# Attention and two mixers on one core: zadd and umm moved ahead of the odd tile's transposes, the last z step one place later, the last output in halves

## The chip, the cores and the metric

One core of a Trainium2 chip runs the whole program once. The metric is device time in microseconds (us) of that core, the median of several executions. The engines are PE (TensorE), VectorE (DVE), ScalarE (ACT), GpSimd (POOL) and SyncE (SP), which mostly issues DMAs. TensorE writes only to PSUM, which this program uses as one tile `ps` of eight banks of 512 float32 columns.

## The reference

Clustered attention, then two mixers. Batch 2, 8 heads, 768 tokens, 64 columns a head.

```python
mask = q_assign[:, :, :, None] == k_assign[:, :, None, :]        # argmax over 16 centroids
scores = np.where(mask, scale * np.matmul(q, k.transpose(0, 1, 3, 2)), -1000000000.0)
attn = np.exp(scores - np.max(scores, axis=-1, keepdims=True))
x = np.matmul(attn / (np.sum(attn, axis=-1, keepdims=True) + 1e-09), v)
# mixer 1: x as (2, 768, 512); U is (768, 32), V (32, 768): a token mix of rank 32
u = x + (x.transpose(0, 2, 1) @ U @ V).transpose(0, 2, 1)
x = u + np.maximum(u @ w_ch1, 0.0) @ w_ch2                       # 512 -> 2048 -> 512
# mixer 2: token mix through 256 with a ReLU, then channels 512 -> 1536 -> 512
u = x + (np.maximum(x.transpose(0, 2, 1) @ w_tok1, 0.0) @ w_tok2).transpose(0, 2, 1)
return u + np.maximum(u @ w_ch1, 0.0) @ w_ch2
```

## The kernel before, in words

Heads go in pairs: 4 pairs in each of 2 batches, 8 groups of 12 tiles, so tiles n = 0 to 95, 128 queries of one head against 768 keys each. The order of the work on each engine is written out by hand: `step(n)` issues the instructions of tile n, and tables (`mid`, `low`, `acts`, `late`) hold what else goes into a step, by tile number. `at(table, n, f)` puts f there. Two tiles, an even and the following odd one, make a pair of steps:

- Even n: score heads of tile n+2 (`s_mm`, four matmuls), `mid`, four of tile n's transposes, VectorE's maximum of tile n+2 (`s_max`), the other two transposes, ScalarE's exponential of tile n+1 (`s_exp`), a copy of four finished transposes to SBUF (`t_out`, ScalarE), `late`.
- Odd n: two transposes, the heads and the maximum of tile n+2, four transposes, `mid`, a `t_out` on VectorE, eight PV matmuls of an earlier half group, `low`, `acts`, the exponential of n+1, a `t_out` on ScalarE, `late`.

Scores lie in banks 0 to 3. Transposes and all extra work take banks 4, 5 and 6 in turn from `ring()`: each taker gets the bank taken three takers before, and must wait until its reader is done. Bank 7 collects PV. `merge` transposes a finished half group back, `merge_out` divides it by its sums into `xn`, the attention's output.

The low-rank token mix of batch 0 is done inside attention of batch 1. `zmm` (tile 59) is x^T U, `zmm_out` copies its four pieces to `z32` (L360), `z_split` makes three parts of it in `zst` (two roundings on ScalarE, L78; one subtraction on VectorE, L85), `zadd` multiplies one block of 128 tokens by V (six blocks, tiles 65, 69, 71, 75, 77, 81), and `zadd_out` adds it to `xn` (L373). `umm` transposes a block of the sum (L377; tiles 83, 87, 89, 93), and `umm_out` splits it into a rounded high part on ScalarE (L78) and the low rest on VectorE (L85): `uh` and `ul`, the input of the channel mixer. `wide` converts weight blocks of the first mixer meanwhile (L96 to L109).

After tile 95 the channel mixer runs in units k: `hidden(k)` (12 matmuls, bank 4 or 5), `hidden_out(k)` (ReLU high part `gh` on ScalarE, low part `gl` on VectorE), `outmm(k)` (12 matmuls into banks 0 to 3). `half_slots` issues hidden(k+1), hidden_out(k+1) and outmm(k) in turn, one slot each. Between the slots `rest_of_u` does the z and u work of the remaining blocks: a list `ops` of pairs (PE part, reader part) which takes banks 6 and 7 in turn. Before the PE part of ops[i] it issues the reader part of ops[i-1]; then it lets some slots pass, by a table of numbers, (1, 1, 2, 2, 1, 1, 1) for the first seven. ops[0] is umm of token block 4, and `zmm` of batch 1 is put in at place 1; its reader part is `z_last` (copies by VectorE and ScalarE in turn, then `z_split`). At the very end `outmm` adds the residual (L750) and sends each of four blocks out by a DMA on SP (L752).

Of the kernel before, what the change touches and what calls it, by code (L numbers as in the profile page):

```python
# [24 lines left out]
def tile_cluster_attention__then__two_mixers(  # L25
# [24 lines left out]
    pe, dve, act, pool, sp = nc.tensor, nc.vector, nc.scalar, nc.gpsimd, nc.sync  # L50
    NB, NPAIR, _, S = qT.shape
# [5 lines left out]
    NC = CD // P  # L57
# [4 lines left out]
    G = NB * NPAIR  # L62
    NTT = 4 * NT
    TW = 512
    NPASS = NB * S // TW
# [6 lines left out]
    def mm(o, l, r, start, stop, **kw):  # L72
        pe.matmul(o, lhsT=l, rhs=r, start=start, stop=stop, **kw)  # L73

    def rnd(eng, o, i, scale=1.0):

        if eng is act:
            act.activation(o, i, AF.Copy, scale=scale)  # L78
        elif eng is dve and scale == 1.0:
            dve.tensor_copy(o, i)  # L80
        else:
            eng.tensor_scalar(out=o, in0=i, scalar1=scale, scalar2=1.0, op0=ALU.mult, op1=ALU.mult)
# [105 lines left out]
    held = {}  # L188
# [115 lines left out]
    def ring():  # L304

        banks.append(banks.pop(0))
        return banks[-1]

    def t_mm(n, c0, c1):
        for c in range(c0, c1):  # L310
            j, i = divmod(NS * n + c, 4)
            if i == 0:
                tb[j] = ring()
            pe.transpose(ps[:, tb[j], ts(i, P)], p32[n % NP32][:, ts(c, P)], ident)  # L314
# [13 lines left out]
    def pv_out(q):  # L328
        act.copy(osb[q % 2], ps[:, OB, 0:HS])

    def merge(q, bk=None):
        held["mg"] = bk = bk or ring()
        for t in range(NT):
            pe.transpose(ps[:, bk, ts(t, P)], osb[q % 2][:, ts(t, P)], ident)  # L334
# [12 lines left out]
    def zmm(gs, bk):  # L347
        held["z"] = bk
        for c in range(NS):
            for i, g in enumerate(gs):  # L350
                b, p = divmod(g, NPAIR)
                mm(ps[R * i : R * i + R, bk, 0:P], u_sb[:, c, :], xn[:, b, p, c, :], c == 0, c == NS - 1)

    def zmm_out(gs, engs):
        for i, g in enumerate(gs):
            z, o = ps[R * i : R * i + R, held["z"], 0:P], z32[:, ts(g % NPAIR, P)]
            if engs[i % 2] is act:
                act.copy(o, z)
            else:
                dve.tensor_copy(o, z)  # L360

    def z_split(gs):
        n, g = len(gs), gs[0]
        z, o = z32[:, g % NPAIR * P : (g % NPAIR + n) * P], zst[:, g * P : (g + n) * P]
        return [lambda: rnd(act, o[0:32], z), lambda: rnd(act, o[32:64], z), lambda: sub(dve, o[64:96], z, f32(o[0:32]))]
# [5 lines left out]
    def zadd_out(b, t, bk):  # L371
        o = xn[:, b, :, t, :]
        dve.tensor_tensor(out=o, in0=ps[:, bk, :].rearrange("p (c k) -> p c k", c=NC), in1=o, op=ALU.add)  # L373
# [5 lines left out]
    def umm_out(b, t, bk):  # L379
        p, k = divmod(b * S + t * P, TW)  # L380
        uh, ul = (x[:, :, k : k + P] for x in fst["u"][p])
        o = ps[:, bk, :].rearrange("p (c k) -> p c k", c=NC)
        return [lambda: rnd(act, uh, o), lambda: sub(dve, ul, o, f32(uh))]
# [178 lines left out]


    NTILE = G * NTT
    mid, low, acts, late = {}, {}, {}, {}

    def at(d, s, f):
        d.setdefault(max(s, 0), []).append(f)

    for g in range(G):  # L570
        s0 = NTT * g
        for h in range(2):
            s = s0 + 2 * NT * h + 4 * NT + 1
            at(mid, s, lambda q=2 * g + h: merge(q))
            at(late, s, lambda q=2 * g + h: merge_out(q))
        n, s1 = g + 1, s0
# [13 lines left out]
            at(late, s1 + 6 if n > 1 else 4, lambda g=n: load_v(g))  # L590

    at(low, 59, lambda: zmm(range(NPAIR), ring()))
    at(late, 60, lambda: zmm_out(range(NPAIR), (dve, dve)))
    for d, s, f in zip((acts, acts, late), (61, 63, 64), z_split(range(NPAIR))):
        at(d, s, f)

    for t in range(NS):
        s = (65, 69, 71, 75, 77, 81)[t]

        def za(t=t):  # L600
            held["za"] = ring()
            zadd(0, t, held["za"])

        at(mid, s, za)
        at(late, s if s == 69 else s + 1, lambda t=t: zadd_out(0, t, held["za"]))
    for s, f in ((0, arg0), (1, lambda: arg1(pool)), (2, arg2), (3, lambda: arg3(pool)), (4, arg4), (5, lambda: mask_rows(pool))):
        at(late, s, f)
    for a in range(2):
# [15 lines left out]
    for t in range(TW // P):  # L624

        def um(t=t):
            held["um"] = ring()
            umm(0, t, held["um"])

        s = NTILE - (13, 9, 7, 3)[t]  # L630
        at(mid, s, um)
        at(acts, s, lambda t=t: umm_out(0, t, held["um"])[0]())
        at(late, s + 1, lambda t=t: umm_out(0, t, held["um"])[1]())

    def step(n):
        k, r = divmod(n, 2 * NT)
        j, i = divmod(NS * n, 4)

        def run(d):
            for f in d.get(n, ()):  # L640
                f()

        def heads():
            if n + 2 < NTILE:
                s_mm(n + 2)

        def maxima():
            if n + 2 < NTILE:
                s_max(n + 2)

        def exps():
            if n + 1 < NTILE:
                s_exp(n + 1)

        def pvs():
            if k:
                pv(k - 1, r - 1)
                pv(k - 1, r)

        def pvo():  # L660
            if k and r == 2 * NT - 1:
                pv_out(k - 1)

        if i == 0:
            heads()
            run(mid)
            t_mm(n, 0, 4)
            maxima()
            t_mm(n, 4, NS)
            exps()  # L670
            t_out(j)
            pvo()
            run(late)
        else:
            t_mm(n, 0, 2)
            heads()
            maxima()
            t_mm(n, 2, NS)
            run(mid)
            t_out(j)  # L680
            pvs()
            run(low)
            run(acts)
            exps()
            t_out(j + 1)
            pvo()
            run(late)
# [41 lines left out]
    def outmm(k):  # L729
        m, p, f = units[k]  # L730
        lo, hi = next(x for x in spans(m, p) if x[0] <= f < x[1])
        wh, wl = (weights(k)[:, 1, j, :] for j in range(2))
        gh, gl = fst["g"][0][k % 2], fst["g"][1][k % 2]
        for c in range(NC):
            o = ps[:, c, :]
            cs = ts(c, P)
            mm(o, wh[:, cs], gh, f == lo, False)
            mm(o, wh[:, cs], gl, False, False)
            mm(o, wl[:, cs], gh, False, f == hi - 1)
        uh, ul = fst["u"][p]  # L740
        if lo == 0 and f == hi - 3:

            for b, s, n, k in pieces(p * TW, TW):
                for c in range(NC):
                    dve.tensor_tensor(out=x2[b][:, c, s : s + n], in0=f32(uh[:, c, k : k + n]), in1=f32(ul[:, c, k : k + n]), op=ALU.add)
        if f == hi - 1:
            for c in range(NC):
                for b, s, n, k in pieces(p * TW, TW):
                    o = x2[b][:, c, s : s + n]
                    dve.tensor_tensor(out=o, in0=ps[:, c, k : k + n], in1=o, op=ALU.add)  # L750
                    if m:
                        sp.dma_start(out[b, c][:, s : s + n], o)  # L752


    def pieces(s0, n, size=S):
        i, k = s0, 0
        while k < n:
            b, s = divmod(i, size)
            w = min(size - s, n - k)
            yield b, s, w, k  # L760
            i, k = i + w, k + w
# [8 lines left out]
    last = 2 * G - 1  # L770
# [5 lines left out]
        pv(last, c)  # L776
    pv_out(last)
    hidden(0, (3,))
    merge(last, 6)
    merge_out(last)  # L780
    ap_ctx.close()

# [88 lines left out]
    def rest_of_u():  # L871


        def z_last(bk):
            gs = range(NPAIR, G)
            zmm_out(gs, (dve, act))
            for f in z_split(gs):
                f()

        def u_out(b, t, bk):  # L880
            for g in umm_out(b, t, bk):
                g()

        u_, z_ = ([(f, o, b, t) for b in range(NB) for t in range(NS)] for f, o in ((umm, u_out), (zadd, zadd_out)))
        ops = []
        order = u_[4:6] + z_[6:8] + u_[6:8]
        for i in range(8, 12):
            order += z_[i : i + 1] + u_[i - 1 : i] * (i > 8)
        order.append(u_[11])
        for f, o, b, t in order:  # L890
            ops.append((lambda bk, f=f, b=b, t=t: f(b, t, bk), lambda bk, o=o, b=b, t=t: o(b, t, bk)))
        ops.insert(1, (lambda bk: zmm(range(NPAIR, G), bk), z_last))
        for i in range(len(ops) + 1):
            if i:
                ops[i - 1][1](6 + (i - 1) % 2)
            if i < len(ops):
                ops[i][0](6 + i % 2)
            for _ in range((1, 1, 2, 2, 1, 1, 1)[i] if i < 7 else 4 if i > 7 else 12):
                yield
# [74 lines left out]
```

## Time and profile before

| | |
|---|---|
| three runs | 768.66, 767.53, 767.29 us; median 767.53 |
| the profiled execution | 767.95 us, its span 766.2 us |
| busy: PE, VectorE, ScalarE, GpSimd | 738.7, 467.1, 310.1, 166.4 us |
| granted TensorE clock | 1.000 of full speed |

In the rows below L73 is the line of all plain matmuls, L314 the transposes of tiles, L334 merge, L377 umm, L292 the maximum, L297 the exponential. A count behind x tells how many instructions a row merges. In a timeline a bracket at the end of a row tells how long the engine was idle before, and what ended that. A row's duration of a few matmuls is longer than the distance to the next row, since matmuls overlap; the chain of waits gives distances.

### The profile page before, as it was taken

To read this page: it belongs to the slowest core of one execution; us is meant where nothing else is said; L and a number is where in the kernel's file an instruction comes from. 1 tells how busy PE (TensorE), PEld (TensorE's weight loads), DVE (VectorE), ACT (ScalarE), POOL (GpSimd) and SP (SyncE) were. 2 spreads that over 40 slices of the span, in tenths; PEclk is the share of its full clock that TensorE was granted. 3 is DMA by queue.
4 is the path that set the end of the run, shared out by engine and by line. 5 is a ranking of instruction groups with operands and counts; after the bars stand their busy time and mean duration, and the time that the engine had idled before them with its cause. 6 is when DMAs were issued, how large, how long until landed. Compare 5 with 4: busy or idle time off the path is not lost.

```text
span 766.2 us, 10466 instructions
## 1 busy us (share of the span) xinstructions
PE 738.7 (96%) x3845; PEld 582.1 (76%) x3845; DVE 467.1 (61%) x689; ACT 310.1 (40%) x565; POOL 166.4 (22%) x147
## 2 busy tenths in 40 slices
PE   1899999999999999999999999999999999999998
PEld 0667766766666688888888888888888888888886
DVE  6778988877777366875758587666675432122113
ACT  3777877867776343332232324323232311111010
POOL 3321432421310122321322122125211410000000
PEclk9999999999999999999999999999999999999999
DMA  5886777875311344753632699967885647555652
GB/s 152 191 185 185 179 186 188 243 183 134 87 63 55 112 165 151 287 193 138 220 131 89 222 346 368 337 238 259 283 286 215 214 144 274 192 192 195 243 192 83
DMA packets 51714, 149.38 MB, mean 195 GB/s; under 512 B 7792, under 2 KB 15984, under 8 KB 49616
## 3 DMA queue, kind: packets, MB, share of 16 engines
q1 hardware_dynamic: 51152, 148.01, 59.7%
q10 hardware_dynamic: 512, 0.72, 0.3%
q8 instruction: 30, 0.49, 0.3%
q14 instruction: 20, 0.16, 0.1%
HBM read 97.32 MB, written 32.51 MB: 169 GB/s over the span
## 4 chain that ended last, share of the span: by engine, by line
PE 92%; DVE 3%; DMA 2%; ACT 2%; issue 1%; SPq 0%; ACTq 0%; DVEq 0%
PE ps L73 82%; PE ps L314 7%; DVE nm L292 1%; DMA xn<-in_U_dram 1%; ACT p L297 1%; ACT qk L78 1%; PE ps L377 1%; PE ps L822 1%; PE ps L334 1%; DMA sq__81<-in_qT_dram 1%; DMA qk<-om 0%; SPq L476 0%; DVE u_sb L100 0%; DVE xn L373 0%; DVE qk L85 0%
## 5 line engine op out<-in xcount | busy, mean ns | idle before, releaser
L727 DVE SCALAR_TENSOR_TENSOR gl<-ps,gh 128x512 fp32r<-128x512 f32 x84 | 58.0, 691 | 209.6 <-ACT gh L726 209.6
L73 PE MATMUL ps<-gh,qk 128*128 128x512 f32 x544 | 179.6, 391 | 0.1
L726 ACT ACTIVATE gh<-ps 128x512 fp32r<-128x512 f32 x84 | 50.2, 598 | 312.9 <-PE ps L73 311.5
L73 PE MATMUL ps<-qk 112*128 112x384 f32 (+2 forms) x456 | 110.8, 370 | 13.0 <-DMA qk<-om 10.3
L73 PEld LDWEIGHTS ps<-gh,qk 128*128 128x128 f32 x544 | 102.1, 188 | 21.6 <-issue 0.5
L292 DVE TENSOR_REDUCE nm<-ps 128x1 f32<-128x768 f32 x96 | 91.8, 956 | 41.5 <-PE ps L73 38.8
L73 PEld LDWEIGHTS ps<-qk 112*128 112x128 f32 (+1 forms) x456 | 77.2, 192 | 44.5 <-issue 20.7
L73 PE MATMUL ps<-gl,qk 128*128 128x512 f32 x272 | 106.1, 390 | 0.0
L85 POOL TENSOR_TENSOR qk<-c__77,qk 128x512 fp32r<-128x512 f32 x40 | 54.9, 1381 | 197.0 <-ACT qk L78 169.1
L297 ACT ACTIVATE p<-ps,nm 128x768 f32<-128x768 f32 x96 | 86.6, 902 | 7.4 <-DVE nm L292 6.8
L314 PE MATMUL ps<-ident,p 128*128 128x128 f32 x576 | 82.1, 275 | 2.6 <-DVE z L360 0.6
L314 PEld LDWEIGHTS ps<-ident,p 128*128 128x128 f32 x576 | 67.6, 140 | 12.8 <-ACT p L297 2.6
L73 PE MATMUL ps<-u2h,qk 128*128 128x512 f32 x224 | 73.9, 391 | 0.0
L73 PE MATMUL ps<-pt,vr 128*64 128x384 f32 x384 | 72.1, 498 | 0.0
L321 ACT COPY pt<-ps 128x512 f32<-128x512 f32 x96 | 56.1, 584 | 35.1 <-PE ps L314 34.7
L73 PEld LDWEIGHTS ps<-gl,qk 128*128 128x128 f32 x272 | 51.1, 188 | 10.2
L73 PE MATMUL ps<-u1h,qk 128*128 128x512 f32 x160 | 52.6, 390 | 0.0
L100 DVE TENSOR_SCALAR c__77<-c__77 128x512 f32<-128x512 f32 (+2 forms) x47 | 49.1, 1045 | 0.8 <-ACT c__77 L96 0.7
L73 PEld LDWEIGHTS ps<-u2h,qk 128*128 128x128 f32 x224 | 42.1, 188 | 8.6
L109 DVE SCALAR_TENSOR_TENSOR c__77<-c__76,c__77 128x512 int32<-128x512 int32 (+2 forms) x47 | 43.4, 923 | 1.5
L106 DVE SCALAR_TENSOR_TENSOR c__77<-c__76,c__77 128x512 int32<-128x512 int32 (+2 forms) x47 | 43.5, 925 | 1.1
L73 PE MATMUL ps<-u2l,qk 128*128 128x512 f32 x112 | 43.6, 390 | 0.0
(146 smaller groups left out, 1017.0 us busy)
## 6 DMA issues: line engine op xcount, KB each, us to landing
qk<-scr_b SPq DMA_DIRECT2D x72, 512.0 KB, 4.2
c__76<-in_wa_dram SPq DMA_DIRECT2D x16, 1024.0 KB, 4.8
qk<-scr_a SPq DMA_DIRECT2D x32, 512.0 KB, 7.6
c__76<-in_wb_dram SPq DMA_DIRECT2D x24, 512.0 KB, 5.1
scr_b<-qk SPq DMA_DIRECT2D x24, 512.0 KB, 4.2
scr_a<-wx SPq DMA_DIRECT2D x16, 512.0 KB, 2.9
scr_a<-qk SPq DMA_DIRECT2D x16, 512.0 KB, 2.7
qk<-sq__81 SPq DMA_DIRECT2D x14, 384.0 KB, 4.0
```

The lines of the kernel that those rows point to most:

```text
L73: pe.matmul(o, lhsT=l, rhs=r, start=start, stop=stop, **kw)
L78: act.activation(o, i, AF.Copy, scale=scale)
L85: eng.tensor_tensor(out=o, in0=a, in1=b, op=ALU.subtract)
L100: dve.tensor_scalar(out=dst, in0=dst, scalar1=2.0 ** -15, scalar2=122879.9921875, op0=ALU.max, op1=ALU.min)
L106: dve.scalar_tensor_tensor(out=d, in0=lo, scalar=29, in1=d, op0=ALU.logical_shift_right, op1=ALU.bitwise_or)
L109: dve.scalar_tensor_tensor(out=d, in0=hi, scalar=-0x40000000, in1=d, op0=ALU.bitwise_and, op1=ALU.bitwise_or)
L292: dve.tensor_reduce(out=nm[:, n % 4 : n % 4 + 1], in_=ps[:, b0 : b0 + 2, 0:HS], axis=AX.XY, op=ALU.max, negate=True)
L297: act.activation(p32[n % NP32].rearrange("p (j k) -> p j k", j=2), ps[:, b0 : b0 + 2, 0:HS], AF.Exp, bias=nm[:, n % 4 : n % 4 + 1], accum_ ...
L314: pe.transpose(ps[:, tb[j], ts(i, P)], p32[n % NP32][:, ts(c, P)], ident)
L321: act.copy(o, ps[:, tb[j], :])
L726: act.activation(gh, o, AF.Relu)
L727: dve.scalar_tensor_tensor(out=gl, in0=o, scalar=0.0, in1=f32(gh), op0=ALU.max, op1=ALU.subtract)
```

## The change

A new table `first` runs at the beginning of an odd step. zadd and umm of batch 0 move there from `mid`, which in an odd step stood behind all transposes. Their VectorE readers move from `late` to `mid` of the next even step, ahead of that step's maximum, and so do the copies after zmm in step 60. The first of z_split's roundings goes from step 61 to 63. The last merge takes bank 0 instead of 6, `zmm` of batch 1 goes to place 2 of `ops`. In the second mixer output DMAs alternate between SP and ScalarE, and the last block of the last pass goes out in two halves.

```diff
-    mid, low, acts, late = {}, {}, {}, {}
+    first, mid, low, acts, late = {}, {}, {}, {}, {}
...
-    at(late, 60, lambda: zmm_out(range(NPAIR), (dve, dve)))
-    for d, s, f in zip((acts, acts, late), (61, 63, 64), z_split(range(NPAIR))):
+    at(mid, 60, lambda: zmm_out(range(NPAIR), (dve, dve)))
+    for d, s, f in zip((acts, acts, late), (63, 63, 64), z_split(range(NPAIR))):
...
-        at(mid, s, za)
-        at(late, s if s == 69 else s + 1, lambda t=t: zadd_out(0, t, held["za"]))
+        at(first, s, za)
+        at(mid, s + 1, lambda t=t: zadd_out(0, t, held["za"]))
...
-        at(mid, s, um)
+        at(first, s, um)
         at(acts, s, lambda t=t: umm_out(0, t, held["um"])[0]())
-        at(late, s + 1, lambda t=t: umm_out(0, t, held["um"])[1]())
+        at(mid, s + 1, lambda t=t: umm_out(0, t, held["um"])[1]())
...
         else:
+            run(first)
             t_mm(n, 0, 2)
...
             for c in range(NC):
-                for b, s, n, k in pieces(p * TW, TW):
+                ends = list(pieces(p * TW, TW))
+                if m and p == NPASS - 1 and c == NC - 1:
+                    ends = [(b, s + i * n // 2, n // 2, k + i * n // 2) for b, s, n, k in ends for i in range(2)]
+                for b, s, n, k in ends:
...
-                        sp.dma_start(out[b, c][:, s : s + n], o)
+                        (sp, act)[(c + k // (TW // 2)) % 2].dma_start(out[b, c][:, s : s + n], o)
...
-    merge(last, 6)
+    merge(last, 0)
...
-        ops.insert(1, (lambda bk: zmm(range(NPAIR, G), bk), z_last))
+        ops.insert(2, (lambda bk: zmm(range(NPAIR, G), bk), z_last))
```

How it moves the instructions, first on PE in tiles 64 and 65 (p_0 and p_1 are their exponentials, zst and vst the operands of zadd):

```order
 L73 MATMUL ps<-qk_73 128x384 x4
 L314 MATMUL ps<-ident,p_0_91 128x128 x6
-L314 MATMUL ps<-ident,p_1_92 128x128 x2
-L73 MATMUL ps<-qk_73 128x384 x4
-L314 MATMUL ps<-ident,p_1_92 128x128 x4
 L73 MATMUL ps<-zst,vst 128x512
+L314 MATMUL ps<-ident,p_1_92 128x128 x2
+L73 MATMUL ps<-qk_73 128x384 x4
+L314 MATMUL ps<-ident,p_1_92 128x128 x4
 L73 MATMUL ps<-pt,vr_89 64x384 x4
```

zadd now stands between the last transpose of the even tile and the first of the odd one; the other five zadds and the four umms move in the same way.

On PE at the end of attention (L334 is the last merge, wx_75 is in hidden(1), xn,u_sb is zmm of batch 1, gh_2241 the beginning of outmm(0)):

```order
 L334 MATMUL ps<-ident,osb_97 128x128 x3
-L377 MATMUL ps<-ident,xn 128x128 x4
+L377 MATMUL ps<-ident,xn 128x128 x8
+L73 MATMUL ps<-qk_72,wx_75 128x512 x12
 L73 MATMUL ps<-xn,u_sb 32x128 x24
-L73 MATMUL ps<-qk_72,wx_75 128x512 x12
-L377 MATMUL ps<-ident,xn 128x128 x4
 L73 MATMUL ps<-gh_2241,wx_74 128x512
```

Two umms now come first, and zmm stands behind hidden(1). What follows on PE is the same in both: outmm(0), hidden(2), zadd of batch 1, outmm(1).

On ScalarE at the same place, before (gh_2241 is the ReLU of hidden_out(0), gh_2242 that of hidden_out(1), then gh_2241 again that of hidden_out(2); L358 are z_last's copies):

```order
L726 ACTIVATE gh_2241<-ps 128x512
L78 ACTIVATE u1h<-ps 128x4x128
L96 ACTIVATE c__77<-c__76 128x1024
L726 ACTIVATE gh_2242<-ps 128x512
L358 COPY z_110<-ps 32x128 x2
L78 ACTIVATE zst<-z_110 32x512 x2
L78 ACTIVATE qk_73<-c__77 128x2x512
L726 ACTIVATE gh_2241<-ps 128x512
```

and with the change:

```order
L727 ACTIVATE gh_2241<-ps 128x512
L78 ACTIVATE u1h<-ps 128x4x128
L96 ACTIVATE c__77<-c__76 128x1024
L727 ACTIVATE gh_2242<-ps 128x512
L78 ACTIVATE u1h<-ps 128x4x128
L78 ACTIVATE qk_73<-c__77 128x2x512
L727 ACTIVATE gh_2241<-ps 128x512
L358 COPY z_110<-ps 32x128 x2
L78 ACTIVATE zst<-z_110 32x512 x2
```

The copies and roundings of z_last stood behind the ReLU of hidden_out(1) and now stand behind that of hidden_out(2); VectorE's part moved in the same way.

## Rows read from the trace of the kernel before

**Rows 1.** The page, busy time of each engine over the span.

```profile
PE 738.7 (96%) x3845; PEld 582.1 (76%) x3845; DVE 467.1 (61%) x689; ACT 310.1 (40%) x565; POOL 166.4 (22%) x147
```

**Rows 2.** Chain of waits, in order of time: start, us, what; opening transposes of four pairs.

```profile
74.82 0.88 PE ps L314 x8
...
153.33 0.87 PE ps L314 x8
...
158.47 0.88 PE ps L314 x8
...
244.75 0.87 PE ps L314 x8
```

**Rows 3.** Chain of waits: matmul pieces between two holes, with their counts.

```profile
160.51 3.81 PE ps L73 x60
...
171.85 2.35 PE ps L73 x12
...
186.00 3.35 PE ps L73 x21
...
191.54 2.57 PE ps L73 x13
...
246.75 0.45 PE ps L377 x4
```

**Rows 4.** Timelines: a hole of PE in tile 61, and VectorE's work before it.

```profile
166.51 0.66 PE L314 MATMUL ps<-ident,p 128*128 128x128 f32 x4 [0.63 <-DVE z L360]
...
165.29 1.17 DVE L360 COPY z<-ps 32x128 f32<-32x128 f32 x4
```

**Rows 5.** Timelines of PE and VectorE in tiles 64 and 70.

```profile
174.03 1.04 PE L314 MATMUL ps<-ident,p 128*128 128x128 f32 x8
...
174.30 0.96 DVE L292 TENSOR_REDUCE nm<-ps 128x1 f32<-128x768 f32 x1 [0.77 <-PE ps L73]
175.29 0.68 DVE L85 TENSOR_TENSOR zst<-z,zst 32x512 fp32r<-32x512 f32 x1
...
189.20 1.20 PE L314 MATMUL ps<-ident,p 128*128 128x128 f32 x8
...
189.03 0.65 DVE L373 TENSOR_TENSOR xn<-ps,xn 128x512 f32<-128x512 f32 x1
```

**Rows 6.** Chain of waits: the transposes of tile 95.

```profile
250.12 0.88 PE ps L314 x6
```

**Rows 7.** Timeline of all engines after attention.

```profile
261.00 0.66 PE L377 MATMUL ps<-ident,xn 128*128 128x128 f32 x4 [0.71 <-DVE xn L342]
...
263.86 0.68 DVE L85 TENSOR_TENSOR u1l<-ps,u1h 128x512 fp32r<-128x512 f32 x1
...
265.89 0.60 PE L377 MATMUL ps<-ident,xn 128*128 128x128 f32 x4
...
266.25 0.48 PE L73 MATMUL ps<-gh,wx 128*128 128x512 f32 x1
...
269.19 0.68 DVE L85 TENSOR_TENSOR zst<-z,zst 32x512 fp32r<-32x512 f32 x1 [0.99 <-ACT zst L78]
...
271.82 0.39 PE L73 MATMUL ps<-zst,vst 96*128 96x512 f32 x1
```

**Rows 8.** PE timeline after two early waits; stretch by engine: busy (count), then granted clock.

```profile
19.03 2.90 PE L73 MATMUL ps<-qk 112*128 112x384 f32 x8 [9.70 <-DMA qk<-om]
...
28.12 0.98 PE L73 MATMUL ps<-qk 128*128 128x384 f32 x4 [1.98 <-ACT p L297]
...
19.00:24.00 5.00, 4.97 (x21) 3.42 (x22) 2.58 (x4) 3.56 (x6) 0.47 (x1) 1.00 0.56 112
```

**Rows 9.** The chain's last row; DMA issues of the output: KB, us to landing.

```profile
762.51 0.69 DVE xn L750
...
out_dram<-xn SPq DMA_DIRECT2D x8, 256.0 KB, 2.1
...
out_dram<-xn SPq DMA_DIRECT2D x8, 128.0 KB, 1.8
```

## The prediction, made before the changed kernel had run

> **What bounds the kernel now.** The page first: PE is busy for 96% of the span, the other engines for 61% at most [rows 1]. So time is won or lost only where PE's order of work has a hole, or where the end hangs on something else. Second the chain of waits, for the 17 pairs of tiles from the opening transposes of tile 58 to those of tile 92: 244.75 - 158.47 = 86.28 us. Tiles 22 to 56 are 17 pairs too, with no z or u work: 153.33 - 74.82 = 78.51 us [rows 2]. They have one set of cluster scores more, 3.35 - 2.57 = 0.78, so plain work is 77.73. To it come, from neighbouring pieces of the chain [rows 3], zmm at 3.81 - 2.35 = 1.46, six zadds at 2.57 - 2.35 = 0.22 and three umms at 0.45: 81.86 us. **The other 4.42 us are holes.** [Rows 4] show one kind: PE waits 0.63 in tile 61 for VectorE's four z copies (1.17 from 165.29), which stood behind a maximum. A second is zadd_out behind other work of VectorE: at 189.20 the transposes of tile 70 open, and a bank of theirs is read until 189.68 [rows 5]. A third kind lies in the umm pairs: ScalarE's rounding waits for a umm that PE reaches last in the odd tile, and the next exponential stands behind it.
>
> Third the timeline of the stretch after attention [rows 7] and the last rows [rows 9].
>
> **The change, part by part.** The sum is made against the profiled execution, 767.95 us (its span is 766.2); the median of the three runs is 767.53, 0.42 lower.
>
> *Pairs 58 to 91.* zadd and umm move ahead of the odd tile's eight transposes and score heads, their VectorE readers ahead of the next even tile's maximum. The bank that the odd tile's last four transposes take was then read in the tile before by a ScalarE copy, long done; umm has its result some 1.5 us earlier (four heads 0.9 [rows 8], six transposes 6/8 of 0.88), so ScalarE rounds while PE goes on. In tile 60 the four z copies start as zmm ends and no longer behind a maximum; that maximum starts a little later, and its exponential is wanted by PE only in tile 62. I take all 4.42 as gone. The lower bound is half of it, were exponentials late instead; there is no more than all of it above.
>
> *Three waits that come instead.* (1) zadd of tile 65 needs the last part of zst, which VectorE still makes after the maximum of tile 66: maximum from 174.30, subtraction 175.29 to 175.97 [rows 5]. PE opens the pair at 174.03 and now reaches zadd after six transposes, at 174.69. It stands until 175.97 + 0.04 = 176.01: **1.32 us**. Behind it stand all PE work and, through the heads, VectorE and ScalarE. (2) zadd_out of tile 69 still stands behind the scores' transpose; it ended at 189.03 + 0.65 = 189.68 [rows 5]. The transposes of tile 70 opened at 189.20 and wanted its bank with the fifth; now the first wants it, so they wait to 189.72, **0.52**. (3) In tile 72 zadd_out stands behind q_lo, which I estimate at **0.2** by the like order of (2). Sum 2.04 (1.3 to 2.6). By the opening of tile 92 the change has won 4.42 - 2.04 = 2.4.
>
> *Tiles 92 to 95.* No heads are left to cover for waits. From 246.75 PE's own work to the opening of tile 95 is umm 0.45, eight PV matmuls 1.45 (the 2.35 of rows 3 less four heads) and six transposes 0.66: 249.31, where the chain has 250.12 [rows 6]. Some 0.15 stays, for the bank that u's low half frees (maximum, copy and subtraction follow each other on VectorE). With the slow restart after the wait (0.88 for six against 0.66) the gain is 0.8, so 3.2 so far (1.0 to 3.9 by the bounds of the 4.42 and of the three waits, one at a time).
>
> *The end of attention* [rows 7]. merge's bank 0 removes the 0.71 that the first umm waited for the merge's reader. But zmm, now third, takes the first umm's bank and waits for u1l, which ends at 263.86 + 0.68 = 264.54, since VectorE's conversions of a weight block stand before it. zmm then runs 264.58 to 266.04, and the first output matmuls start at 266.04 instead of 266.25: 0.2 won.
>
> The other side of this edit is the largest single term. z_last (four copies, two roundings, a subtraction) now stands behind hidden_out(2) on both engines, and zadd of batch 1 stands on PE right behind hidden(2), ahead of outmm(1). So PE must stand from the end of hidden(2) until hidden_out(2) **and** z_last are done. Before, the same chain hung on hidden(1): from 265.89, when PE was done with it, to 269.19 + 0.68 + 0.04 = 269.91, **4.02 us**; it was hidden by outmm(0) and hidden(2), 5.57 us of PE work. That cover is gone. I see nothing on the queues that shortens or lengthens it much (3.7 to 4.4). hidden(2) ends 0.2 earlier for the gain at zmm, so zadd starts at 271.82 - 0.21 + 4.02 = 275.63 against 271.82: **3.8 lost** after this place. From there on the order is the same, and PE has no slack to win anything back.
>
> *The end* [rows 9]. Two half sums pay the start of an instruction twice and so end a little later than one whole of 0.69, I take 0.1, and a 128 KB piece lands in 1.8 after its issue, a 256 KB one in 2.1: 0.2 won (0 to 0.4). The Trainium skill (Trainium Kernel Development and Optimization, Key Constraints) says that DMAs from several queues share the same 16 engines and save only the issue time; by that rule this term is nearer 0, and the sum 0.2 higher. The other output DMAs on ScalarE wait for sums that end while PE does the next hidden matmuls, whose ReLU is the next thing on that queue: nothing. On SP only the output issues are fewer; its loads keep their order.
>
> Sum: -3.2 + 3.8 - 0.2 = **+0.4** (the 0.2 won at zmm is in the 3.8), so 768.35 for an execution like the profiled one, **767.9** at the median. A measurement of this kernel can tell about 0.2% (1.5 us) from no change; this is within it.
>
> **The rivals.**
>
> *Slower: PE comes out of the 4 us stand at half pace.* After its 9.70 us wait at the start PE took 2.90 us for eight matmuls of the kind that went four in 0.98 after a wait of 1.98, and 4.97 us for 21 matmuls [rows 8], where 21 like ones took 3.35 [rows 3]: 1.6 us lost. The granted clock reads 1.00 (2.4 GHz) there, but the pace is that of the lower level, 1.2 GHz. A stand of 4.02 lies nearer to 1.98 than to 9.70, so this is not the likeliest. It decides if PE falls after a stand somewhere between the two. Time: 767.9 + 1.6 = 769.5. The Trainium skill (TensorE: Matmul & The Clock Gate, HAM oscillation) warns that waits of a matmul stream for its data let the array's clock be throttled again, and tells of a kernel where each such wait did so; by it this rival would be the forecast. The trace agrees for 9.70 and shows nothing between.
>
> *Slower: the reordered VectorE queue only trades waits.* If the earlier sums delay maxima and with them exponentials, half of the 4.42 stays: 767.9 + 2.2 = 770.1. Against it: the maximum that starts later is an even tile's, and its exponential is wanted only after the rest of the pair's work and the next heads. That includes the case that the change doesn't do what it says; at tile 69 it does not, the reader keeps its place.
>
> *Faster: VectorE gets ahead.* If VectorE, with readers done early, came to its queue's next work sooner than I reckon, most of waits (1) to (3) would vanish, 1.5 us, and if the four z copies, which take 1.17 on one engine [rows 4], ran in two pairs side by side in z_last, 0.6 of the 4.02 would go too: 767.9 - 2.1 = 765.8. Against: wait (1) hangs on a maximum that hangs on PE itself, and in both kernels the copies of z_last take turns on the two engines.
>
> **How the numbers follow.** Forecast 0.55, with a range of its own of 766.6 to 769.0 from the bounds of its terms; PE at half pace 0.27; traded waits 0.06; faster 0.12. Of the forecast's share 0.04 lies beyond 0.2% slower (769.06), and of the half-pace case 0.06 within it; of the faster case 0.02 stays above 766.0. So slower 0.31, within 0.59, faster 0.10. The range 766.3 to 769.8 leaves out some 0.1 on each side.
>
> **What would show it.** Right: PE's transposes in the odd tiles without VectorE waits, tile 92 opened 2 to 3 us earlier against tile 58; a PE wait of about 1.3 for zst in tile 65 and 0.5 in tile 70; a PE wait of about 4.0 between hidden(2) and zadd of batch 1, one of the three longest of the kernel; the last output landing 0.2 earlier. Wrong: no wait at zadd of batch 1 (then 764), or matmuls behind it that take twice as long (then 769.5).

## The result, and the profile after

| | before | changed |
|---|---|---|
| median of six runs each, in turns | 767.35 us (766.90 to 768.66) | **771.54 us** (770.46 to 772.66) |
| ratio | | **1.0052, interval 1.0039 to 1.0065** |
| profiled execution, its span | 767.95, 766.2 us | 770.79, 769.0 us |

The change makes the kernel 4.2 us (0.5%) slower. Forecast was 767.9, "within 0.2%", and the range of 766.3 to 769.8 does not hold the result. The page hides all of it: the busy times [rows 1] are what they were.

```profile
PE 739.1 (96%) x3845; PEld 584.2 (76%) x3845; DVE 468.8 (61%) x690; ACT 310.6 (40%) x565; POOL 167.6 (22%) x147
```

So the difference has to be looked for in PE's order of work, stretch by stretch. The two traces side by side, in us; tile 58 is taken at its opening transposes, hidden(n) and outmm(n) at their first matmul in PE's timeline:

| stretch | before | changed | difference | predicted |
|---|---|---|---|---|
| start to tile 58 | 158.31 | 157.94 | -0.37 | 0 |
| tile 58 to tile 92 (chain of waits) | 86.28 | 84.68 | -1.60 | -2.4 |
| tile 92 to hidden(0) | 7.78 | 6.95 | -0.83 | -0.8 |
| hidden(0) to outmm(0) | 13.88 | 13.62 | -0.26 | -0.2 |
| outmm(0) to zadd of batch 1 | 5.57 | 9.70 | +4.13 | +4.02 |
| that zadd to hidden(3) | 2.95 | 4.64 | **+1.69** | **0** |
| hidden(3) to the end of the span | 491.43 | 491.47 | +0.04 | -0.2 |
| sum (the spans) | 766.2 | 769.0 | +2.8 | +0.4 |

(The third row is the rest of tile 58 to hidden(0), 94.06 against 91.63.) One row stands at nothing in the forecast's sum; it was the price of a rival. Here is what stands behind each.

Three of the waits of PE in the changed kernel (engine, what it waited for, us in total, times, the longest):

```profile
PE ps L73 <- DVE zst L85: 5.2, 2, 4.0
...
PE ps L314 <- DVE xn L373: 1.0, 2, 0.6
PE ps L73 <- DVE u1l L85: 0.6, 1, 0.6
```

The line of 5.2 us is new, and its 4.0 is one wait. In attention the chain of waits opens tiles 58 and 92 at

```profile
158.10 0.88 PE ps L314 x8
...
242.78 0.66 PE ps L314 x6
```

against [rows 2], and the three new waits stand in PE's timeline in tiles 65, 70 and 72 (start, us, instructions merged; in the bracket the idle time before and what ended it):

```profile
174.90 0.47 PE L73 MATMUL ps<-zst,vst 96*128 96x512 f32 x1 [1.27 <-DVE zst L85]
...
189.66 0.87 PE L314 MATMUL ps<-ident,p 128*128 128x128 f32 x6 [0.38 <-DVE xn L373]
...
195.57 0.66 PE L314 MATMUL ps<-ident,p 128*128 128x128 f32 x4 [0.63 <-DVE xn L373]
```

They were forecast at 1.32, 0.52 and 0.2. PE's timeline shows no other wait between tile 58 and the end of attention. After attention the same timeline answers to [rows 7]:

```profile
263.19 0.50 PE L73 MATMUL ps<-gh,wx 128*128 128x512 f32 x1
...
266.05 2.88 PE L73 MATMUL ps<-qk 128*128 128x512 f32 x12
272.89 0.47 PE L73 MATMUL ps<-zst,vst 96*128 96x512 f32 x1 [3.96 <-DVE zst L85]
273.19 0.40 PE L73 MATMUL ps<-gh,wx 128*128 128x512 f32 x1
...
273.66 0.93 PE L73 MATMUL ps<-gh,wx 128*128 128x512 f32 x2
274.39 0.63 PE L73 MATMUL ps<-gl,wx 128*128 128x512 f32 x1
...
277.53 2.91 PE L73 MATMUL ps<-qk,qk 128*128 128x512 f32 x12
```

hidden(2) runs from 266.05; then PE stands for 3.96 us until zadd. The chain of waits names what it stands for, in order of time: hidden_out(2) on ScalarE and VectorE, then z_last, link by link.

```profile
268.96 0.61 ACT gh L727
...
269.59 0.69 DVE gl L728
270.28 0.20 DVE z L360
...
271.40 0.64 ACT zst L78
...
272.06 0.69 DVE zst L85
```

PE is back at work at 272.89. The pair of matmuls from 273.66 is the first that takes longer (0.93 us, where such a pair took 0.62 to 0.63 before), and from then on one matmul of 512 columns takes 0.63 in place of 0.39. So the pace fell some 0.9 us after the restart. The stretches show why (busy us and count of PE, PEld, VectorE, ScalarE, GpSimd; then the granted clock, the DMA share and GB/s):

```profile
270.00:272.00 2.00, 0.00 (x0) 0.00 (x0) 0.75 (x3) 1.11 (x3) 0.00 (x0) 1.00 0.00 0
272.00:274.00 2.00, 1.11 (x5) 0.91 (x6) 1.91 (x2) 0.66 (x2) 0.00 (x0) 0.95 0.00 0
274.00:276.00 2.00, 2.00 (x6) 1.61 (x5) 1.22 (x1) 0.00 (x0) 0.00 (x0) 0.50 0.00 0
276.00:278.00 2.00, 2.00 (x7) 1.54 (x7) 0.00 (x0) 0.00 (x0) 0.00 (x0) 0.70 0.91 229
```

The granted clock is 0.50, that is 1.2 in place of 2.4 GHz, while PE is fully busy: six matmuls in a slice in which ten fit at full clock. That is the +1.69.

At the end, the last five sums (three whole ones and the two halves) and the DMA issues of the two halves (instructions, KB, us from issue to landing) answer to [rows 9]:

```profile
763.26 2.79 DVE L754 TENSOR_TENSOR xn<-ps,xn 128x512 f32<-128x512 f32 x5 [2.08 <-PE ps L73]
```

```profile
out_dram<-xn ACTq DMA_DIRECT2D x1, 128.0 KB, 2.1
out_dram<-xn SPq DMA_DIRECT2D x1, 128.0 KB, 2.1
```

The two half sums together end at 766.05, 0.78 us behind PE's last matmul, where the whole one ended 0.72 behind it (763.20 - 762.48). Each half lands 2.1 us after its issue, as a whole block of 256 KB did; the 1.8 of [rows 9] is that of other 128 KB pieces. From PE's last matmul to the end of the span it is 766.2 - 762.48 = 3.7 before and 769.0 - 765.27 = 3.7 after.

### The profile page after: what moved, and what is told of

Same layout as the page of the kernel before. It is cut to its first block, busy times and chain, and to the rows that moved or that the text cites. A ratio compares the mean times of both kernels' runs of the same rounds, so it can differ in the third digit from the quotient of the medians.

```text
span 769.0 us, 10472 instructions
## 1 busy us (share of the span) xinstructions
PE 739.1 (96%) x3845; PEld 584.2 (76%) x3845; DVE 468.8 (61%) x690; ACT 310.6 (40%) x565; POOL 167.6 (22%) x147
## 4 chain that ended last, share of the span: by engine, by line
PE 92%; DVE 3%; DMA 2%; ACT 1%; issue 1%; SPq 0%; ACTq 0%; DVEq 0%
PE ps L73 82%; PE ps L314 7%; DVE nm L292 1%; DMA xn<-in_U_dram 1%; PE ps L826 1%; PE ps L334 1%; DMA sq__81<-in_qT_dram 1%; PE ps L377 1%; ACT p L297 1%; DMA qk<-om 1%; ACT qk L78 0%; DVE sq__81 L241 0%; SPq L476 0%; DVE pt L319 0%; DVE zst L85 0%
## 5 line engine op out<-in xcount | busy, mean ns | idle before, releaser
L85 POOL TENSOR_TENSOR qk<-c__77,qk 128x512 fp32r<-128x512 f32 x40 | 55.4, 1394 | 198.1 <-ACT qk L78 170.2
```

The costliest lines, as they stand in the source:

```text
L85: eng.tensor_tensor(out=o, in0=a, in1=b, op=ALU.subtract)
```

## The experiments

Theory A: the loss is the 4 us stand at zadd of batch 1, which the third place of zmm makes, and the half clock right behind it; the attention part wins some 2.4. Rivals: the loss or the half clock come from the reordered odd tiles or from the output; or the clock falls wherever PE stands, in some executions. Ratios are to the kernel before, run in turns on the same chip (medians 767.9 to 768.0). Where nothing else is said, an edit is shown against the changed kernel.

### zmm of batch 1 back in second place

```diff
-        ops.insert(2, (lambda bk: zmm(range(NPAIR, G), bk), z_last))
+        ops.insert(1, (lambda bk: zmm(range(NPAIR, G), bk), z_last))
```

> The changed kernel with one thing put back: zmm and z_last of batch 1 stand second among the small jobs again, all else of the change stays. Theory A (the loss is the 4.0 us stand of PE at zadd of batch 1, and the half clock right behind it): the stand is gone, hidden(2) covers the chain of z_last, no granted clock of 0.50 from 272 to 278, and about 2.4 us of the attention part remain won, with the 0.3 won at the merge bank: 767.35 - 2.7 = 764.7 (764.0 to 765.3). Theory B (the loss and the fall of the clock come from the rest: the reordered odd tiles, or the output halves on two queues): no faster than 767.4, or a clock that falls all the same. Theory C (the half clock comes in some executions wherever PE happens to stand): a run or a trace with a mean clock under 0.998.

Measured: 764.52 us, ratio 0.9949 [0.9936, 0.9962]. PE goes from hidden(2) into zadd without a wait, and on to hidden(3):

```profile
267.76 2.88 PE L73 MATMUL ps<-qk 128*128 128x512 f32 x12
270.48 0.39 PE L73 MATMUL ps<-zst,vst 96*128 96x512 f32 x1
...
273.43 2.88 PE L73 MATMUL ps<-qk,qk 128*128 128x512 f32 x12
```

One edit in one line turns +4.2 into -3.5. The rivals that put the loss into the odd tiles or the output fall, for both are still there. The profiled run of this kernel was its slowest, though (766.67; the others 763.6 to 764.5), and that speaks to theory C: in its trace PE waited 2.02 us at 44 us for a DMA, and behind that the clock was 0.59 and 0.56 (its PE timeline, then its stretches):

```profile
46.33 1.60 PE L73 MATMUL ps<-qk 112*128 112x384 f32 x4 [2.02 <-DMA qk<-om]
```

```profile
46.00:48.00 2.00, 1.68 (x6) 1.61 (x7) 0.00 (x0) 0.00 (x0) 0.00 (x0) 0.59 0.58 78
48.00:50.00 2.00, 2.00 (x11) 2.00 (x10) 1.42 (x2) 1.18 (x3) 0.46 (x1) 0.56 0.87 299
```

So the clock can fall elsewhere too, at the same kind of place (PE stands, then starts), in some executions; in the kernel before this wait was 0.55 in its trace.

### The reader of zmm issued ahead of hidden(2)

```diff
         for i in range(len(ops) + 1):
-            if i:
+            if i and i != 3:
                 ops[i - 1][1](6 + (i - 1) % 2)
...
-            for _ in range((1, 1, 2, 2, 1, 1, 1)[i] if i < 7 else 4 if i > 7 else 12):
+            for j in range((1, 1, 2, 2, 1, 1, 1)[i] if i < 7 else 4 if i > 7 else 12):
+                if i == 2 and j == 1:
+                    ops[2][1](6)
```

> The changed kernel, zmm still third, but its reader z_last issued between outmm(0) and hidden(2), ahead of hidden_out(2), instead of behind it. zadd of batch 1 then has hidden(2), about 2.85 us of PE work, beside the chain of z_last (copies, roundings and the subtraction, some 2.5 to 3.2 us once the converters are free). Theory A (the place of the reader makes the stand): a stand of 0 to 0.8 at zadd and no fall of the clock, 764.5 to 766.0, with a possible new wait of hidden(3) for hidden_out(2) that now comes later. Theory B (zmm as third is itself the cost, whatever its reader does): 767 or more.

Measured: 765.03 us, ratio 0.9963 [0.9951, 0.9975]. zmm is still third and still waits 0.56 for u1l, but z_last now runs beside hidden(2): its last subtraction starts at 266.91, and zadd follows hidden(2) without a wait.

```profile
265.73 2.88 PE L73 MATMUL ps<-qk 128*128 128x512 f32 x12
268.45 0.39 PE L73 MATMUL ps<-zst,vst 96*128 96x512 f32 x1
...
266.91 0.69 DVE L85 TENSOR_TENSOR zst<-z,zst 32x512 fp32r<-32x512 f32 x1 [0.99 <-ACT zst L78]
```

What makes the stand is therefore not where zmm stands on PE, but that its reader stands behind hidden_out(2) while zadd stands right behind hidden(2). The place of zmm itself costs 0.6: from hidden(0) to outmm(0) it takes 13.62 here and 12.98 with zmm second.

### Extra matmuls in the stand: 16, 9 and 4

```diff
             if i == 3:
+                for _ in range(16):
+                    mm(ps[:, 4, :], weights(2)[:, 0, 0, 0:P], fst["u"][0][0][:, 0, :], True, True)
```

(9 and 4 in the other two.) These three measure the half clock by itself: the stand's place and zadd's start stay, and only PE's idle time in between gets shorter.

> The changed kernel with 16 extra matmuls of 512 columns (about 3.4 to 3.5 us at full pace) put between hidden(2) and zadd of batch 1, into a bank that is free there; their results are never read, so the output is as before. They add no time of their own as long as they fit in the stand. Theory A (the half clock follows from PE standing idle): the stand shrinks to some 0.5, the granted clock stays 1.00, outmm(1) takes 2.7 again instead of 4.34, and the time falls by 1.6 to 771.5 - 1.6 = 769.9, with zadd starting no earlier than in the changed kernel. Rival (the clock falls for another reason at that place, the load of work so far or the bank): outmm(1) still takes over 4 us, and the time stays at 771.5 or above it.

> The changed kernel with 9 extra matmuls of 512 columns (9 x 0.22 = 1.95) between hidden(2) and zadd of batch 1, results never read, output as before. The stand left is about 4.0 - 1.95 = 2.0; the first job ends on the same VectorE chain, so PE starts again at the same time as in the changed kernel. If the clock falls only after a stand clearly longer than 2: clock 1.00 throughout, outmm(1) in 2.7, 769.3 like the kernel with 16 (769.3). If any stand of about 2 us is enough at this place: 0.50 in the rows behind it, 771 to 772. My own reading leans to the first (0.7), since the wait of 1.98 at the start kept its pace in the kernel before.

> The changed kernel with 4 extra matmuls of 512 columns (4 x 0.22 = 0.87) at the same place, output as before: a stand of about 3.1 us is left. If the clock falls here too, time and pace are those of the changed kernel (771.5, outmm(1) 4.3); if not, 769.3. I lean to the fall (0.6).

| extra matmuls | stand | zadd to hidden(3) | granted clock 274 to 276 | span | median (lowest to highest, runs) | ratio to the kernel before | runs with a mean clock of 0.998 or less |
|---|---|---|---|---|---|---|---|
| 0 (the change) | 3.96 | 4.64 | 0.50 | 769.0 | 771.54 (770.46 to 772.66, 6) | 1.0052 [1.0039, 1.0065] | 6 of 6 |
| 4 | 3.06 | 4.65 | 0.59 | 769.5 | 770.48 (769.65 to 772.29, 9) | 1.0033 [1.0021, 1.0044] | 6 of 9 |
| 9 | 1.93 | 3.05 | 1.00 | 767.5 | 770.36 (768.77 to 773.84, 12) | 1.0030 [1.0018, 1.0043] | 6 of 12 |
| 16 | 0.35 | 3.07 | 1.00 | 767.6 | 769.28 (768.59 to 772.20, 12) | 1.0021 [1.0013, 1.0030] | 2 of 12 |

The stretches behind the restart, with 16, 9 and 4 extra matmuls (the third figure from the end is the granted clock):

```profile
274.00:276.00 2.00, 2.00 (x10) 1.62 (x10) 1.39 (x2) 0.00 (x0) 0.00 (x0) 1.00 0.00 0
```

```profile
274.00:276.00 2.00, 2.00 (x10) 1.66 (x9) 1.30 (x2) 0.00 (x0) 0.00 (x0) 1.00 0.00 0
```

```profile
274.00:276.00 2.00, 2.00 (x7) 1.56 (x6) 1.77 (x2) 0.00 (x0) 0.00 (x0) 0.59 0.00 0
```

With 16 more matmuls, worth 3.6 us of PE's time, the kernel is **2.3 us faster** (771.54 to 769.28; 2.4 by the ratios) although zadd starts no earlier: the half clock follows from PE's standing. In the traces a stand of 3.06 at this place brought it and one of 1.93 did not; with 9 my forecast of the trace came true, that of the median (769.3) did not. With 9 matmuls six of the twelve runs show a mean clock of 0.998 or less, and take 770.3 to 773.8; with 4, three of nine show 0.999 and take 769.7 to 770.0. In the kernel before, which has no stand there, six of 49 runs show 0.998 or less. Only the profiled runs have a trace, so where the clock fell in each of the others stays open.

The traces do show that the length of a stand does not decide alone. Near the start of the kernel PE waits once or twice for 1 to 2 us. In the kernel before it did so for 1.98 at 28.12 us, and the clock read 1.00 in all of the next 6 us. In the last version below (output whole) it waited at the same place, for 1.97, and the clock fell to half (its PE timeline, then a stretch):

```profile
27.68 0.97 PE L73 MATMUL ps<-qk 128*128 128x384 f32 x4 [1.97 <-ACT p L297]
```

```profile
30.00:32.00 2.00, 2.00 (x9) 1.90 (x8) 1.36 (x2) 0.77 (x3) 1.24 (x3) 0.50 0.93 204
```

Of the eight stands of 1.86 to 2.02 us in all traces, three brought a half clock (1.87, 1.97 and 2.02) and five did not (1.86, 1.88, 1.93, 1.96 and 1.98); the seven of 1.06 to 1.64 at 28 us and the 0.35 at zadd did not either, and the four of 3.06 and more behind hidden(2) all did. What decides near 2 us, no run here shows.

### The kernel before with zmm third, and nothing else

```diff
-        ops.insert(1, (lambda bk: zmm(range(NPAIR, G), bk), z_last))
+        ops.insert(2, (lambda bk: zmm(range(NPAIR, G), bk), z_last))
```

> The kernel before with a single thing of the change: zmm and z_last of batch 1 stand third among the small jobs. Theory A: the stand of some 4 us at zadd and the half clock behind it (1.6) come in full, no gain of the attention part: 767.4 + 4.0 + 1.6 - 0.2 = 772.8 (771.5 to 774). Theory B (the loss comes from the rest of the change): within 0.5 of the kernel before.

Measured: 774.11 us, ratio 1.0078 [1.0066, 1.0090], 6.1 us slower than before, 1.3 more than I expected and just outside my range. The stand is 3.97, but here the clock fell during it, so zadd and nearly all of outmm(1) ran at half pace (stretches, then PE's timeline):

```profile
272.00:274.00 2.00, 0.00 (x0) 0.00 (x0) 1.16 (x3) 0.71 (x3) 0.00 (x0) 0.90 0.00 0
274.00:276.00 2.00, 0.42 (x1) 0.45 (x2) 1.22 (x2) 1.32 (x3) 0.00 (x0) 0.50 0.00 0
276.00:278.00 2.00, 2.00 (x6) 1.52 (x6) 1.92 (x2) 0.00 (x0) 0.00 (x0) 0.50 0.00 0
```

```profile
275.58 0.77 PE L73 MATMUL ps<-zst,vst 96*128 96x512 f32 x1 [3.97 <-DVE zst L85]
```

From zadd to hidden(3) it takes 280.90 - 275.58 = 5.32, which is 2.37 above the 2.95 of before, not 1.69. With the stand's 4.2 (outmm(0) at 265.84 to zadd, 9.74 against 5.57) that is 6.5; the spans, 772.3 and 766.2, differ by 6.1, since tile 58 opens 0.35 earlier here. The one line thus brings the whole loss, without the attention part and without the output.

### The changed kernel once more

No edit: a second trace, to see whether the spread of its runs has the same source.

> The changed kernel itself once more, for the spread of its runs. In its first trace PE restarted at full clock and fell to 0.50 about 0.9 us later (1.62 lost in outmm(1)); in the kernel with zmm third and nothing else the clock had fallen during the stand, and outmm(1) lost 2.60. If the spread from 770.5 to 772.7 comes from when the clock falls against the restart, this trace again shows outmm(1) at 4.3 to 5.4 instead of 2.7, and its span goes with it, 769.0 plus what outmm(1) takes beyond 4.34. If the spread has another source, outmm(1) stays at 4.3 while the time differs by a microsecond or more.

Measured: 771.89 us, ratio 1.0044 [1.0027, 1.0061], span 770.4. This time the clock is down before PE is back (0.56 in the stretch with the restart at 273.17; it was 0.95 there in the first trace), zadd itself takes 0.77, and hidden(3) starts at 278.85:

```profile
272.00:274.00 2.00, 0.83 (x2) 0.77 (x3) 1.63 (x2) 0.94 (x2) 0.00 (x0) 0.56 0.00 0
```

```profile
273.17 0.77 PE L73 MATMUL ps<-zst,vst 96*128 96x512 f32 x1 [3.97 <-DVE zst L85]
...
278.85 3.02 PE L73 MATMUL ps<-qk,qk 128*128 128x512 f32 x12
```

zadd to hidden(3) takes 5.68, 1.04 more than in the first trace; outmm(1) alone takes 278.85 - 273.73 = 5.12, within the 4.3 to 5.4. (The 2.60 in my expectation is not right: with zmm third and nothing else outmm(1) lost 280.90 - 276.15 - 2.72 = 2.03.) The span is 1.4 longer, and 0.26 of the rest lies before tile 58. So the half clock costs 1.69 in one execution and 2.73 in another, by when it falls against the restart. The second is the one that adds up to the difference of the medians: -2.42 in attention, -0.26, +4.14 and +2.73 make +4.19, and 771.54 - 767.35 = 4.19. These are two traces; the runs beside them, up to 773.59, have none.

### The attention part alone

The kernel before with the tables and the step of the change (zmm_out, z_split, zadd, umm and their readers, and the new list first); merge's bank, zmm's place and the output are as before (part of the edit, against the kernel before).

```diff
+            run(first)
             t_mm(n, 0, 2)
...
-        at(mid, s, za)
-        at(late, s if s == 69 else s + 1, lambda t=t: zadd_out(0, t, held["za"]))
+        at(first, s, za)
+        at(mid, s + 1, lambda t=t: zadd_out(0, t, held["za"]))
```

> The kernel before with the attention part of the change alone (sums and transposed rows open the odd tile, readers as the even tile opens); the merge bank, the place of zmm and the output are as before. By the trace of the changed kernel this part is worth 2.43 us from tile 58 to the first hidden matmul: 768.0 - 2.4 = 765.6 (765.0 to 766.2). The 0.7 of the first umm behind the merge's reader stays, which is the difference to the run with zmm put back second (764.5). If the attention part were worth nothing, 767.5 to 768.5.

Measured: 765.27 us, ratio 0.9960 [0.9946, 0.9973]; tile 58 to hidden(0) is 249.13 - 157.49 = 91.64, as in the changed kernel, with the same three waits (1.26, 0.38, 0.63). This part wins what its trace says.

### A version without the waits

```diff
-        ops.insert(2, (lambda bk: zmm(range(NPAIR, G), bk), z_last))
+        ops.insert(1, (lambda bk: zmm(range(NPAIR, G), bk), z_last))
...
-    for d, s, f in zip((acts, acts, late), (63, 63, 64), z_split(range(NPAIR))):
+    for d, s, f in zip((acts, acts, late), (61, 61, 62), z_split(range(NPAIR))):
...
-        at(mid, s + 1, lambda t=t: zadd_out(0, t, held["za"]))
+        at(acts if s in (69, 71) else mid, s if s in (69, 71) else s + 1, lambda t=t: zadd_out(0, t, held["za"]))
```

> The changed kernel with zmm of batch 1 second again, the parts of zst made a tile pair earlier (roundings at 61, subtraction at 62), and the zadd_outs of tiles 69 and 71 read in their own tile, ahead of the next tile's scores' transpose and q_lo. Theory A (the waits 1.27, 0.38 and 0.63 that took the place of the old ones are PE time one for one): PE has no wait at zadd of tile 65 nor at the transposes of tiles 70 and 72, tile 58 to the first hidden matmul 2.3 shorter than in the changed kernel, and 764.5 - 2.0 = 762.5 (761.9 to 763.3). Rival (VectorE's chain of maxima and exponentials is the true limit there, so a wait removed comes back as a wait for p): 764 or more, with new waits of PE for p or pt.

Measured: **761.68 us, ratio 0.9914 [0.9900, 0.9928]**, and 761.80 when run again (0.9914 [0.9891, 0.9937]): 6.3 and 6.1 us faster than the kernel before, 0.2 and 0.1 better than the lower end of what I expected. PE has no wait for VectorE from tile 58 to the end of attention, and the chain of waits opens tiles 58 and 92 at

```profile
157.41 0.88 PE ps L314 x8
...
239.29 0.66 PE ps L314 x6
```

That is 81.88 us; the forecast's sum of plain work from [rows 2, 3] was 81.86. The changed kernel took 84.68, so its three waits cost 2.80 of PE's time, more than the 2.28 in their brackets, and VectorE's chain of maxima has room for all of it.

### The output whole again, on one queue

The version without the waits, with and without the halves.

```diff
-                if m and p == NPASS - 1 and c == NC - 1:
+                if False:
...
-                        (sp, act)[(c + k // (TW // 2)) % 2].dma_start(out[b, c][:, s : s + n], o)
+                        sp.dma_start(out[b, c][:, s : s + n], o)
```

> The version with none of the waits (zmm second, zst earlier, two zadd_outs in their own tile), but each output whole and on SyncE as in the kernel before, to price the output halves and the second queue by themselves. By the traces (last matmul to the end of the span 3.7 in both) the halves are worth nothing: 761.7 like the version with halves, within 0.3. By my prediction's term they would be worth 0.2; that they cost something is the rival (761.3 or less).

> The version with none of the waits once more, with halves, on the same chip as the one with whole outputs: 761.7 (761.0 to 762.5) against 767.9 of the kernel before, and the partner for pricing the halves.

Measured: 761.70 whole (0.9915 [0.9893, 0.9937]), 761.80 in halves. From PE's last matmul to the end of the span: 760.4 - 756.72 = 3.7 whole, 762.3 - 758.53 = 3.8 in halves. The medians (each known to some 1.8 us against the kernel before) could not show a difference of 0.2; the traces show none.

## Why the prediction was wrong, and where it was right

**The step that failed** is one choice: "A stand of 4.02 lies nearer to 1.98 than to 9.70, so this is not the likeliest." The stand itself was forecast in its place and size (4.02, found 3.96, 3.97 and 3.97), and so was the mechanism of the rival, half pace behind it. But I chose between two rows by their distance, where the trace of before gives no reason that the effect should go by distance. After 4 us the clock was at 0.50 in all three traces that have such a stand, and after 3.06 too. Nor is 1.98 a length that keeps the clock: 1.97 at the same place lost it in another kernel's trace. With the choice went a term that the sum left at nothing, zadd to hidden(3), which measured +1.69 and +2.73. The rule of the Trainium skill (TensorE: Matmul & The Clock Gate, HAM oscillation) that I set beside it, that a matmul stream which waits for its data is throttled again, made this the forecast; the traces agree for the stands of 3.06 and above, and for three of the eight near 2.

**The rival's price** was too small as well: 1.6 against 1.69 in one trace and 2.73 in the other. (The 21 matmuls of its two rows are not all of the same kinds; kind by kind, in PE's timeline, the sixteen ahead of the next heads lose 2.83 - 1.64 and 1.30 - 0.79, that is 1.7. And at that place the clock reads 1.00, so no row shows that the slow pace there had the same cause.) With 2.73, and with 0.8 and 0.2 from the terms below, 767.9 + 2.7 + 0.8 + 0.2 is 771.6, where 771.54 was measured.

**The attention term** had the right holes and the wrong sum. The 4.42 us of holes are real: without any wait the 17 pairs take 81.88. But the waits that came instead cost 84.68 - 81.88 = 2.80, not 2.04. Measured from tile 58 against the version without them, PE is 1.50 later behind the wait in tile 65, 0.58 more behind that of tile 70 and 0.71 more behind that of tile 72, where 1.32, 0.52 and 0.2 were forecast; the brackets (1.27, 0.38, 0.63) count idle time only, from the end of the row before. The wait of tile 72 was the bad guess: zadd_out stands there behind a q_lo that took 1.62, where the same operation took 0.95 before (the last section has the rows). Tiles 92 to 95 came as worked out (0.83 for 0.8).

**zmm and merge** (0.26 for 0.2) and **the stand** came as worked out. **The output** did not: 0.2 was expected, nothing came. The term took its 1.8 us from 128 KB pieces elsewhere in the kernel; the halves at the end landed in 2.1, as a whole block did, and from the last sum to the end of the span it is 3.0 in both. The traces agree here with the rule that I quoted against the term (the Trainium skill, Trainium Kernel Development and Optimization, Key Constraints: several queues share the same DMA engines and save issue time alone).

**The other rivals.** "Trades waits" and "VectorE gets ahead" are both out: the attention part keeps its gain in every kernel that has it, and the waits at tiles 65, 70 and 72 and at zadd of batch 1 stand where they were put. The faster case's idea that the four copies might run in pairs is out too: they took turns, from 270.20 to 271.37.

## What to carry to other kernels

When a change takes away the work that covered a chain of readers, price the stand of PE and, behind it, some microseconds of matmuls at half clock (1.7 to 2.7 us lost here behind a stand of 4; near 2 us it came in some executions and not in others). Move the reader together with the producer: issuing z_last one place earlier was worth 6.5 us (771.54 to 765.03). Before a wait is accepted as the price of a better order, ask whether its producer can start a step sooner: of the three new waits none was needed, and without them, and with zmm back in second place, the same change is 6.2 us faster than the kernel before.

## What the runs showed of the hardware that I had not expected

The clock need not be down when PE comes back. In the first trace of the changed kernel PE ran at full pace for 0.9 us (zadd, then matmuls of 0.40 from 273.19) and then fell to half while fully busy; in the second trace it was at half from the first matmul. The same program thus differs by 1.0 us from run to run at one place.

VectorE and GpSimd took turns. In the changed kernel q_lo on VectorE came 0.6 us later than before, and began just behind a product on GpSimd (L213), with k_lo (GpSimd, L85) next:

```profile
193.29 1.62 DVE L241 SCALAR_TENSOR_TENSOR sq__81<-sq__81 128x768 fp32r<-128x768 f32 x1
...
193.19 0.91 POOL L213 TENSOR_TENSOR am<-am,wcl 128x384 bf16<-128x384 bf16 x1
194.06 2.53 POOL L85 TENSOR_TENSOR sk__82<-sk__82 128x768 fp32r<-128x768 f32 x1
```

In the kernel before it was q_lo that came first, and the product that took longer:

```profile
192.68 0.95 DVE L241 SCALAR_TENSOR_TENSOR sq__81<-sq__81 128x768 fp32r<-128x768 f32 x1
...
193.27 1.14 POOL L213 TENSOR_TENSOR am<-am,wcl 128x384 bf16<-128x384 bf16 x1
194.37 1.83 POOL L85 TENSOR_TENSOR sk__82<-sk__82 128x768 fp32r<-128x768 f32 x1
```

The rows read as one waiting for the other's end: the product ends at 193.19 + 0.91 = 194.10, and q_lo ends 0.81 behind that, at 194.91, where it takes 0.95 alone. In the three traces of the version without the waits (two with halves, one with the output whole) q_lo began some 0.13 later behind the product than here, and took 1.50 in place of 1.62: again it ended 0.81 to 0.82 behind the product's end. So its duration goes by when the product ends and not by its own start. The Trainium skill (SBUF — State Buffer, SBUF: two separate sides) says that VectorE and GpSimd share a pair of ports as an exclusive lock, which a VectorE operation with two SBUF inputs takes against a GpSimd one that reads SBUF; q_lo has two, and the durations agree. No run took the overlap away, so this cause is argued and not shown. The 0.7 us that q_lo loses here is more than the whole wait of tile 72 (0.63), and my 0.2 for that wait did not have it.

Work that nobody reads can make a kernel faster: 16 matmuls in the stand won 2.3 us; in the trace the clock stayed at 1.00.
